# Delta-rule recurrence in chunks: three tiles for a's rows, and the preparation of the next chunks at another place in the order

## The chip, the cores and the metric

One core of a Trainium2 chip runs the whole program. The metric is the device time of one execution in microseconds (us), as the median of several runs. The engines are named as in the profile: PE (TensorE, with PEld for its weight loads), DVE (VectorE), ACT (ScalarE), POOL (GpSimd), SP (SyncE). SP's queue issues nearly all DMAs, one after the other: a DMA that waits for its buffer holds up those that stand behind it.

## The reference

```python
for t in range(S):                       # S = 768, 4 x 8 heads, head size 40
    y[:, :, t] = einsum('bhd,bhde->bhe', r_t, state)
    Sa = einsum('bhde,bhe->bhd', state, a_t)
    state = state * w_t[:, :, None, :] - einsum('bhd,bhe->bhde', Sa, b_t) \
          + einsum('bhd,bhe->bhde', v_t, k_t)
...
x = _moe_ref(y, ...)      # y as [4, 768, 320]: gelu, norm, a 768 x 768 mix over time, gate, + x
return _moe2_ref(x, ...)  # relu, a convolution of width 3, sigmoid gate, projection
```

All of it is float32. The change touches the recurrence alone (`_attn_ref`).

## The kernel before, in words

The recurrence is cut into 12 chunks of 64 steps. A chunk (`hg` in the code) is worked on for all 32 heads at once; the two halves of the heads (`q` = 0, 1) are independent chains. Two chunks make a group `g`, so there are six groups, and the loop over `g` at the end of `_attention` is the place of the change.

What is done for a chunk:

- `prep(hg)` loads a's rows (`at`, 1 MB), the rows of k and b (`kbt`, 1 MB) and the decays, makes running products of the decays by scans (L100, L103 on DVE), and scales `at` (L105, DVE) and `kbt` (L107, POOL) with them.
- `products(hg)` multiplies `kbt` by `at` on PE (`gk`, L129), masks the result into the tile `la` (L132, DVE), transposes `kbt` on PE (`pkb`, L135), copies that out (L136, ACT), and copies a part of `la` on POOL (L140).
- `solve_a(g)` inverts the triangular 32x32 blocks of both chunks of a group on DVE: two transposes of `la` into `mu` (L164), 30 steps of a multiplication and an addition that depend on each other (L171, L173), and two transposes out (`tn` L177, `tt` L179). These are called here solve 0 to solve 5. A solve needs `la` of both of its chunks.
- `solve_b(g, tq)` finishes the inverse for one chunk on PE (`pn` L192, `pt` L204, both of 32x32 tiles) and ACT (`n1` L198, `tt` L209), and at its end copies `at` into `la` (L210). Only then is that chunk's `at` tile free.
- `chain(g, c)` carries the state through one chunk and one half of the heads: `py` L227, `pz` L234, `pS` L243 and L246, `pzt` L255 on PE, with short copies on ACT (L231, L237, L258) and DVE (L236, L251, L252) between. `chain 2` needs `chain 0`, `chain 3` needs `chain 1`.
- `spart` transposes the state (`p` L265). `ypart` makes the output of one chunk and half: `gh` L279 and `pyo` L288, L290 on PE, `ghs` L283 and `xo` L293 on DVE, then the DMA to `x_attn`. `prep_y` and `prep_v` load what these need (`r`, `zv`, `vz`).

The list `ORDER` gives for every group in which order these pieces are written: `a` is a part of the next group's solve (three of the 30 steps), `b0`, `b1` the two `solve_b` of the next group, `p0`, `p1` and `g0`, `g1` `prep` and `products` of the two chunks of the group after the next, `sp` and `y` the parts of the same name, `py` a `prep_v`. A scheduler then orders the instructions of each engine by its own clock; of those that are ready it takes the higher `level` first (chains 3; a, b, sp, p and g 2; y 0). On each engine the instructions then run strictly in that order.

The tiles that matter: `at` comes from the pool `e2` with two buffers, `mu` and `n1` from `e1` with one each, `la` is a pair (`la_103`, `la_104`) that the groups use in turn. So `prep` of a chunk can load `at` only when `solve_b` of the chunk two before it has copied its own out.

After the six groups the rest of the network follows from about 770 us on; it isn't touched.

Of the kernel before, what the change touches and what calls it, by code (L numbers as in the profile page):

```python
# [10 lines left out]
F32 = mybir.dt.float32  # L11
# [16 lines left out]
def _attention(ctx, tc, ident, gu, wp, wr, a, kb, r, vt, v, x):  # L28
# [6 lines left out]
    D, C, J = 40, 64, 4  # L35
# [11 lines left out]
    e1 = early.enter_context(tc.tile_pool(name="a_e1", bufs=1, side="right"))  # L47
    e2 = early.enter_context(tc.tile_pool(name="a_e2", bufs=2, side="right"))
# [30 lines left out]
    def flat(t):  # L79
        return t.rearrange("p n t -> p (n t)")  # L80

    def prep(hg):

        at = e2.tile([128, 16, 2, C], F32, name="at")
        kbt = e1.tile([128, 16, 2, C], F32, name="kbt")
        px = p4.tile([128, 16, 65], F32, name="px")
        ws = [[], []]
        for q in range(2):
            for i, src in enumerate((wp, wr)):
                t = e2.tile([128, 8, 65], F32, name=f"w{i}")  # L90
                nc.sync.dma_start(out=flat(t), in_=src[hg, :, 520 * q:520 * q + 520])
                ws[q].append(t)
            if q == 0:
                nc.sync.dma_start(out=at.rearrange("p n P t -> p (n P t)"), in_=a[hg])
                nc.sync.dma_start(out=kbt.rearrange("p n c t -> p (n c t)"), in_=kb[hg])
        for q in range(2):
            ns = slice(8 * q, 8 * q + 8)
            w1, w2 = ws[q]
            nc.vector.memset(first[:, :, 0], 1.0)  # L99
            nc.vector.tensor_tensor_scan(out=flat(px[:, ns]), data0=flat(w1), data1=flat(first), initial=0.0,  # L100
                                         op0=ALU.mult, op1=ALU.add)
            nc.vector.reciprocal(first[:, :, 0], px[:, ns, 64])
            nc.vector.tensor_tensor_scan(out=flat(w2), data0=flat(w2), data1=flat(first), initial=0.0,  # L103
                                         op0=ALU.mult, op1=ALU.add)
            nc.vector.tensor_tensor(out=at[:, ns], in0=at[:, ns], in1=px[:, ns, None, 0:C].to_broadcast([128, 8, 2, C]),  # L105
                                    op=ALU.mult)
            nc.gpsimd.tensor_tensor(out=kbt[:, ns], in0=kbt[:, ns],  # L107
                                    in1=w2[:, :, C - 1::-1][:, :, None, :].to_broadcast([128, 8, 2, C]), op=ALU.mult)
            for i, t in enumerate((flat(px[:, ns]), flat(w2))):
                junk = e1.tile([128, 8 * 65], F16, name="junk")  # L110
                u = 4 * hg + 2 * q + i
                nc.scalar.activation(out=junk, in_=t, func=AF.Square, scale=2.0 ** -32, accum_out=gu[:, u:u + 1])
        tl[hg] = dict(px=px, at=at, kbt=kbt)
# [70 lines left out]
    def solve_b(g, tq):  # L184

        la, tt, tn = (grp[g][n] for n in ("la", "tt", "tn"))
        cs = slice(4 * tq, 4 * tq + 4)
        pn = ps_a.tile([128, 4, J, 32], F32, name="pn", tag="pa")
        for c in range(4):
            for j in range(J):  # L190
                for P in range(2):
                    nc.tensor.matmul(out=pn[rq(2 * P + 1), c, j], lhsT=la[rq(2 * P), P, 4 * tq + c, j, 32:64],  # L192
                                     rhs=tn[rq(2 * P), 4 * tq + c, j], start=True, stop=True,
                                     tile_position=(64 * P, 64 * P + 32))
        n1 = e1.tile([128, 4, J, 32], F32, name="n1")
        for P in range(2):
            i1 = rq(2 * P + 1)
            nc.scalar.activation(out=n1[i1], in_=pn[i1], func=AF.Copy)  # L198
        pt = ps_a.tile([128, 4, J, 32], F32, name="pt", tag="pa")
        for c in range(4):  # L200
            for j in range(J):
                for P in range(2):
                    i0, i1 = rq(2 * P), rq(2 * P + 1)
                    nc.tensor.matmul(out=pt[i0, c, j], lhsT=n1[i1, c, j], rhs=tt[i1, 4 * tq + c, j, 32:64],  # L204
                                     start=True, stop=True, tile_position=(64 * P + 32, 64 * P))
        at = tl[2 * g + tq]["at"]
        for P in range(2):
            i0 = rq(2 * P)
            nc.scalar.activation(out=tt[i0, cs, :, 32:64], in_=pt[i0], func=AF.Copy)  # L209
            nc.scalar.activation(out=la[half[P], P, cs].rearrange("p c j t -> p (c j) t"), in_=at[half[P], :, P],  # L210
                                 func=AF.Copy, scale=-1.0)
# [59 lines left out]
    def ypart(g, c4):  # L271
        hg, q = 2 * g + c4 // 2, c4 % 2
        d = tl[hg]
        kbn, px, (r2, zv) = d["kbn"], d["px"], rv[2 * hg + q]
        pyo = ps_a.tile([128, 8, C], F32, name="pyo", tag="pa")
        for s in range(2):
            gh = ps_g.tile([128, J, 2, C], F32, name="gh", tag="pg")
            for j in range(J):
                nc.tensor.matmul(out=gh[:, j].rearrange("p P t -> p (P t)"),  # L279
                                 lhsT=zv[:, 4 * s + j].rearrange("p c t -> p (c t)"),  # L280
                                 rhs=r2[:, 4 * s + j].rearrange("p P t -> p (P t)"), start=True, stop=True)
            ghs = p2.tile([128, J, 2, C], F32, name="ghs")
            nc.vector.tensor_tensor(out=ghs, in0=gh, in1=m8, op=ALU.mult)  # L283
            for j in range(J):
                for P in range(2):
                    i = 4 * s + j
                    if hg > 0:
                        nc.tensor.matmul(out=pyo[half[P], i], lhsT=s0s[hg, q][:, D * i:D * i + 64], rhs=r2[:, i, P],  # L288
                                         start=True, stop=False)
                    nc.tensor.matmul(out=pyo[half[P], i], lhsT=kbn[:, 8 * q + i, P], rhs=ghs[:, j, P],  # L290
                                     start=(hg == 0), stop=True)
        xo = p2.tile([128, 2, J, C], F32, name="xo")
        nc.vector.tensor_tensor(out=xo.rearrange("p s j t -> p (s j) t"), in0=pyo, in1=px[:, 8 * q:8 * q + 8, 0:C],  # L293
                                op=ALU.mult)
        for s in range(2):
            xv = x[2 * q + s, :, C * hg:C * hg + C].rearrange("(j P e) t -> P e j t", j=J, P=2)
            for P in range(2):
                nc.sync.dma_start(out=xv[P], in_=xo[real[P], s])

    def level(n):  # L300
        return tc.high_priority(offset=100000 * n)
# [16 lines left out]
    for hg in (2, 3):  # L318
        prep(hg)
        products(hg)  # L320
    ORDER = ["chain 0", "chain 1", "a", "a", "sp 0", "a", "y 0", "a", "a", "sp 1", "a", "py0", "y 1", "a", "a", "chain 2",
             "chain 3", "a", "a", "a", "b0", "p0", "sp 2", "y 2", "b1", "py1", "g0", "sp 3", "y 3", "p1", "g1"]
    for g in range(NG):
        n1, n2 = g + 1 < NG, g + 2 < NG
        sa = solve_a(g + 1) if n1 else iter(())
        if not n1:
            early.close()
        for it in ORDER:
            if it == "a":
                with level(2): next(sa, None)  # L330
            elif it in ("b0", "b1"):
                if n1:
                    with level(2):
                        run(sa)
                        solve_b(g + 1, int(it[1]))
            elif it in ("p0", "p1"):
                if n2:
                    with level(2): prep(2 * g + 4 + int(it[1]))
            elif it in ("g0", "g1"):
                if n2:  # L340
                    with level(2): products(2 * g + 4 + int(it[1]))
            elif it in ("py0", "py1"):
                if n1: prep_v(2 * g + 2 + int(it[2]))
            else:
                what, c = it.split()
                c = int(c)
                last = 2 * g + c // 2 == NH - 1
                if what == "chain":
                    with level(3): chain(g, c)
                    if not n1 and c == 1:  # L350
                        yield
                elif what == "sp":
                    if not last:
                        with level(2): spart(g, c)
                else:
                    ypart(g, c)
                    if 4 * g + c + 3 < 2 * NH: prep_y(4 * g + c + 3)


# [443 lines left out]
```

## Time and profile before

| | |
|---|---|
| median of 3 runs | 1268.96 us (1262.32 to 1287.53) |
| the profiled execution | 1269.13 us, of which the span from first to last instruction is 1267.4 us |
| busy share of the span | PE 76%, PEld 69%, DVE 58%, ACT 34%, POOL 18% |
| mean granted PE clock | 0.793 of full |
| recurrence | about 0 to 770 us |

The profile shows one execution on the engines' common time axis. A row of the timeline gives start, duration, engine, line, operation, the tiles as out<-in, the count of equal instructions merged, and in brackets the idle time of that engine just before and what ended it. A matmul of float32 appears twice in the counts of the trace (two passes). The clock PEclk is the share of PE's full clock that was granted, at either of two levels, 1.2 and 2.4 GHz.

### The profile page before, as it was taken

Reading aid. Unit: us, or ns where it says so; the run is one execution under the profiler, and the core shown is the slowest. Engines: PE = TensorE matmul, PEld = TensorE weight load, DVE = VectorE, ACT = ScalarE, POOL = GpSimd, SP = SyncE. Lnnn points to the kernel's source line nnn. Section 1 sums busy time; section 2 is a strip of 40 time slices with the busy share of each in tenths; the row PEclk is TensorE's granted clock in tenths of the full one; section 3 lists DMA queues with packets and bytes.
Section 4 is the critical chain, followed back from the end, with each engine's and each line's share of the span. In section 5 each row is a group of like instructions: output and inputs, shape, how many; then the busy total and the mean of one; then the engine's idle time right before and its main releaser. Section 6 shows DMA issues by size and latency. Waiting matters only on the chain.

```text
span 1267.4 us, 23131 instructions
## 1 busy us (share of the span) xinstructions
PE 957.5 (76%) x9777; PEld 870.8 (69%) x9777; DVE 730.5 (58%) x1323; ACT 429.2 (34%) x833; POOL 228.4 (18%) x213
## 2 busy tenths in 40 slices
PE   3218719990997399819994886589999978899995
PEld 3217717880776288717883785589999968799994
DVE  5873682189247622772285534285555668767763
ACT  2214212230432213212221423242222336777763
POOL 4300210021101100220020101230111143333331
PEclk8658955685878557855885588989999989899997
DMA  9302501352235113510430327200000121000000
GB/s 307 123 16 105 162 27 35 108 161 76 76 116 162 59 35 114 155 47 32 137 95 28 118 72 218 70 27 1 1 1 1 34 74 60 16 17 32 17 18 33
DMA packets 47490, 94.49 MB, mean 75 GB/s; under 512 B 20240, under 2 KB 26384, under 8 KB 44304
## 3 DMA queue, kind: packets, MB, share of 16 engines
q1 hardware_dynamic: 47376, 92.91, 23.2%
q8 instruction: 79, 1.29, 0.4%
q14 instruction: 35, 0.29, 0.1%
HBM read 85.02 MB, written 7.86 MB: 73 GB/s over the span
## 4 chain that ended last, share of the span: by engine, by line
PE 26%; DVE 11%; DMA 7%; ACT 6%; issue 3%; POOL 3%; SPq 0%; DVEq 0%; POOLq 0%; ACTq 0%
PE pv L612 5%; PE pr L633 3%; DMA raw<-in_moe_w_in 2%; PE pq L703 2%; PE pu L594 2%; DMA raw<-in_moe_w_out 2%; PE ph L563 2%; POOL cv L689 2%; DVE cv L684 2%; DVE gl L693 2%; ACT cv L683 1%; DVE cv L686 1%; DMA raw<-in_moe_w_sg 1%; PE gk L129 1%; PE p L680 1%
## 5 line engine op out<-in xcount | busy, mean ns | idle before, releaser
L192 PE MATMUL pn<-tn,la 32*32 32x32 f32 x768 | 35.0, 234 | 173.7 <-DVE tn L177 173.7
L192 PEld LDWEIGHTS pn<-tn,la 32*32 32x32 f32 x768 | 26.8, 145 | 184.3 <-issue 163.0
L129 PE MATMUL gk<-at,kbt 128*128 128x128 f32 x384 | 89.2, 372 | 32.3 <-POOL kbt L107 22.2
L129 PEld LDWEIGHTS gk<-at,kbt 128*128 128x128 f32 x384 | 69.4, 256 | 43.5 <-POOL kbt L107 26.6
L107 POOL TENSOR_TENSOR kbt<-kbt,w 128x1024 f32<-128x1024 f32 x24 | 56.3, 2351 | 235.3 <-DVE first L99 139.9
L689 POOL TENSOR_TENSOR cv<-cv,hz 128x384 f32<-128x384 f32 x64 | 61.8, 974 | 123.5 <-ACT cv L688 123.5
L171 DVE TENSOR_TENSOR mtmp<-mu 128x30 f32<-128x30 f32 (+9 forms) x180 | 74.2, 412 | 5.3
L132 DVE TENSOR_TENSOR la<-gk,minus 128x512 f32<-128x512 f32 x48 | 32.9, 685 | 72.9 <-PE gk L129 72.9
L210 ACT ACTIVATE la<-at 64x1024 f32<-64x1024 f32 x24 | 25.3, 1054 | 143.1 <-issue 104.0
L105 DVE TENSOR_TENSOR at<-at,px 128x1024 f32<-128x1024 f32 x24 | 35.2, 1488 | 52.0 <-DMA at<-in_c_a 52.0
L612 PE MATMUL pv<-sg_hi,vh 128*128 128x384 f32 x192 | 64.4, 336 | 0.4 <-ACT vh L586 0.4
L612 PE MATMUL pv<-sg_lo,vh 128*128 128x384 f32 x192 | 64.4, 335 | 0.0
L173 DVE TENSOR_TENSOR mu<-mu,mtmp 128x30 f32<-128x30 f32 (+9 forms) x180 | 61.2, 340 | 5.3
L612 PE MATMUL pv<-sg_hi,vl 128*128 128x384 f32 x192 | 64.1, 335 | 0.0
L290 PE MATMUL pyo<-ghs,kbn 128*64 128x64 f32 x768 | 62.3, 245 | 2.1 <-DVE ghs L283 2.1
L258 ACT ACTIVATE zv<-pzt 64x512 f32<-64x512 f32 x48 | 28.3, 590 | 102.8 <-PE pzt L255 68.4
L255 PE MATMUL pzt<-tt,ys 128*128 128x64 f32 x384 | 60.8, 323 | 1.6 <-ACT s L268 1.6
L288 PE MATMUL pyo<-r,s 128*64 128x64 f32 x704 | 61.6, 251 | 0.0
L616 POOL TENSOR_TENSOR g<-g,u 128x384 f32<-128x384 f32 x32 | 35.2, 1103 | 140.1 <-DVE g L615 138.4
L255 PEld LDWEIGHTS pzt<-tt,ys 128*128 128x128 f32 x384 | 56.9, 234 | 4.4 <-ACT s L268 2.2
L703 PE MATMUL pq<-wv_hi,gh 128*128 128x320 f32 x192 | 42.3, 328 | 23.0 <-ACT gh L692 23.0
L290 PEld LDWEIGHTS pyo<-ghs,kbn 128*64 128x64 f32 x768 | 53.9, 158 | 5.9 <-DVE ghs L283 2.9
(149 smaller groups left out, 2469.1 us busy)
## 6 DMA issues: line engine op xcount, KB each, us to landing
at<-in_c_a SPq DMA_DIRECT2D x12, 1024.0 KB
kbt<-in_c_kb SPq DMA_DIRECT2D x12, 1024.0 KB
zv<-in_c_vt SPq DMA_DIRECT2D x24, 512.0 KB
r<-in_c_r SPq DMA_DIRECT2D x24, 512.0 KB
w<-in_c_wp SPq DMA_DIRECT2D x24, 260.0 KB
w<-in_c_wr SPq DMA_DIRECT2D x24, 260.0 KB
raw<-in_moe_w_in SPq DMA_DIRECT2D x8, 512.0 KB
vz<-in_c_v SPq DMA_DIRECT2D x24, 160.0 KB
```

Of the source, the lines that this page charges most:

```text
L107: nc.gpsimd.tensor_tensor(out=kbt[:, ns], in0=kbt[:, ns], in1=w2[:, :, C - 1::-1][:, :, None, :].to_broadcast([128, 8, 2, C]), op=ALU.mult)
L129: nc.tensor.matmul(out=pg[:, j].rearrange("p P t -> p (P t)"), lhsT=kbt[:, n].rearrange("p c t -> p (c t)"), rhs=at[:, n].rearrange("p P t ...
L171: nc.vector.tensor_tensor(out=tv, in0=mu[:, j + 1:32, j:j + 1].to_broadcast([128, n, j]), in1=mu[:, j:j + 1, 0:j].to_broadcast([128, n, j] ...
L173: nc.vector.tensor_tensor(out=mu[:, j + 1:32, 0:j], in0=mu[:, j + 1:32, 0:j], in1=tv, op=ALU.add)
L192: nc.tensor.matmul(out=pn[rq(2 * P + 1), c, j], lhsT=la[rq(2 * P), P, 4 * tq + c, j, 32:64], rhs=tn[rq(2 * P), 4 * tq + c, j], start=True, ...
L255: nc.tensor.matmul(out=pzt[:, i], lhsT=ys[:, i].rearrange("p P e -> p (P e)"), rhs=tt[:, 2 * c4 + i // 4, i % 4], start=True, stop=True)
L288: nc.tensor.matmul(out=pyo[half[P], i], lhsT=s0s[hg, q][:, D * i:D * i + 64], rhs=r2[:, i, P], start=True, stop=False)
L290: nc.tensor.matmul(out=pyo[half[P], i], lhsT=kbn[:, 8 * q + i, P], rhs=ghs[:, j, P], start=(hg == 0), stop=True)
L612: nc.tensor.matmul(out=po, lhsT=l[:, fs], rhs=rr[:, k, cs], start=(n == 0), stop=(n == 3 * NT - 1))
L633: nc.tensor.matmul(out=po, lhsT=ww[:, k, ms], rhs=ghl[k][i], start=(n == 0), stop=(n == 3 * NF1 - 1))
L689: nc.gpsimd.tensor_tensor(out=cv, in0=cv, in1=h[:, 1:N2 + 1], op=ALU.mult)
L703: nc.tensor.matmul(out=po, lhsT=gs[k][g][:, ts], rhs=rr[:, k], start=(n == 0), stop=(n == 3 * NF2 - 1))
```

## The change

`at` gets three buffers. `n1` gives up its own buffer and takes `mu`'s. In `ORDER` the first preparation of the group after the next (`p0`, `g0`) moves from behind the solve to its middle, before and behind chains 2 and 3; the second (`p1`) now follows `b0`, and `b1` comes last but one. `ypart` gets level 1 instead of 0.

```diff
-        at = e2.tile([128, 16, 2, C], F32, name="at")
+        at = e2.tile([128, 16, 2, C], F32, name="at", bufs=3)
...
-        n1 = e1.tile([128, 4, J, 32], F32, name="n1")
+        n1 = e1.tile([128, 4, J, 32], F32, name="n1", tag="mu")
...
-    ORDER = ["chain 0", "chain 1", "a", "a", "sp 0", "a", "y 0", "a", "a", "sp 1", "a", "py0", "y 1", "a", "a", "chain 2",
-             "chain 3", "a", "a", "a", "b0", "p0", "sp 2", "y 2", "b1", "py1", "g0", "sp 3", "y 3", "p1", "g1"]
+    ORDER = ["chain 0", "chain 1", "a", "a", "sp 0", "a", "y 0", "a", "a", "sp 1", "a", "py0", "y 1", "a", "p0", "chain 2",
+             "chain 3", "g0", "a", "a", "a", "a", "sp 2", "y 2", "b0", "p1", "sp 3", "py1", "y 3", "b1", "g1"]
...
-                    ypart(g, c)
+                    with level(1): ypart(g, c)
```

What the scheduler makes of it, at three places that repeat in each group.

First the stretch between two solves, here the one that follows solve 3. On PE, before, the 32x32 products `pn` of the second `solve_b` and the 128x128 products `gk` stand in turn, ahead of chain 1's `pz`:

```order
L227 MATMUL py<-vz,la_104 64x40 x16
L192 MATMUL pn<-tn,la_104 32x32 x6
L129 MATMUL gk<-at,kbt 128x128
L192 MATMUL pn<-tn,la_104 32x32
L129 MATMUL gk<-at,kbt 128x128
L192 MATMUL pn<-tn,la_104 32x32
L129 MATMUL gk<-at,kbt 128x128
L192 MATMUL pn<-tn,la_104 32x32
L129 MATMUL gk<-at,kbt 128x128
L192 MATMUL pn<-tn,la_104 32x32 x7
L129 MATMUL gk<-at,kbt 128x128
L234 MATMUL pz<-ys_106,tt_100 64x40 x16
```

On PE, now, at the same place:

```order
L255 MATMUL pzt<-tt_100,ys_105 128x64 x8
L192 MATMUL pn<-tn,la_104 32x32 x5
L246 MATMUL pS<-vz,kbn 64x40
L227 MATMUL py<-vz,la_104 64x40 x16
L246 MATMUL pS<-vz,kbn 64x40 x15
L192 MATMUL pn<-tn,la_104 32x32 x2
L234 MATMUL pz<-ys_106,tt_100 64x40
L192 MATMUL pn<-tn,la_104 32x32
L234 MATMUL pz<-ys_106,tt_100 64x40 x15
L243 MATMUL pS<-st_110,ident 64x320 x2
```

No `gk` stands there any more: 16 of the 32 `gk` of a group have moved into the solve before.

On DVE, in the same stretch, before, from chain 1's last copy to the scans of the second `prep`:

```order
L252 TENSOR_TENSOR st_110<-pS,px 128x320
L293 TENSOR_TENSOR xo<-pyo,px 128x512
L283 TENSOR_TENSOR ghs<-gh,mask 128x512 x2
L236 COPY vz<-pz 64x320
L251 TENSOR_TENSOR vz<-pS,px 64x320 x2
L252 TENSOR_TENSOR st_109<-pS,px 128x320
L293 TENSOR_TENSOR xo<-pyo,px 128x512
L100 SCALAR_TENSOR_TENSOR px<-w_3496,first 128x520
L102 RECIPROCAL first<-px 128x8
L105 TENSOR_TENSOR at<-at,px 128x1024
```

On DVE, now:

```order
L252 TENSOR_TENSOR st_110<-pS,px 128x320
L293 TENSOR_TENSOR xo<-pyo,px 128x512
L100 SCALAR_TENSOR_TENSOR px<-w_3345,first 128x520
L102 RECIPROCAL first<-px 128x8
L105 TENSOR_TENSOR at<-at,px 128x1024
```

One output part and chain 2's copies no longer stand ahead of the scans (L100).

Second the solve, on DVE. Before, its later steps follow each other:

```order
L171 TENSOR_TENSOR mtmp<-mu 128x238
L173 TENSOR_TENSOR mu<-mu,mtmp 128x14x17
L171 TENSOR_TENSOR mtmp<-mu 128x234
L173 TENSOR_TENSOR mu<-mu,mtmp 128x13x18
L171 TENSOR_TENSOR mtmp<-mu 128x228
```

Now, at the same steps:

```order
L171 TENSOR_TENSOR mtmp<-mu 128x238
L132 TENSOR_TENSOR la_104<-gk,minus 128x4x2x64
L173 TENSOR_TENSOR mu<-mu,mtmp 128x14x17
L171 TENSOR_TENSOR mtmp<-mu 128x234
L173 TENSOR_TENSOR mu<-mu,mtmp 128x13x18
L171 TENSOR_TENSOR mtmp<-mu 128x228
L132 TENSOR_TENSOR la_104<-gk,minus 128x4x2x64
```

Four of a group's eight `la` (L132) stand among the steps of the solve before, and wait there for `gk`; chain 3's copies, two L105, two more L283 and one more L293 do so too.

Third SP's queue. Before, both loads of `at` stand together, ahead of the second chunk's `kbt`:

```order
L91 DMA w_3504<-in_c_wr 128x520
L94 DMA at<-in_c_a 128x2048 x2
L146 DMA vz<-in_c_v 64x640 x2
L156 DMA r_3287<-in_c_r 128x1024
L298 DMA x_attn<-xo 40x4x64 x4
L155 DMA zv<-in_c_vt 128x1024
L95 DMA kbt<-in_c_kb 128x2048
```

Now, the second `at` and the `kbt` of the chunk that is prepared in the solve stand behind `r`, an output and the decays:

```order
L298 DMA x_attn<-xo 40x4x64 x4
L94 DMA at<-in_c_a 128x2048
L146 DMA vz<-in_c_v 64x640 x2
L156 DMA r_3449<-in_c_r 128x1024
L94 DMA at<-in_c_a 128x2048
L298 DMA x_attn<-xo 40x4x64
L91 DMA w_3919<-in_c_wp 128x520
L298 DMA x_attn<-xo 40x4x64 x3
L91 DMA w_3925<-in_c_wp 128x520
L91 DMA w_3921<-in_c_wr 128x520
L91 DMA w_3927<-in_c_wr 128x520
L95 DMA kbt<-in_c_kb 128x2048
```

The load of `r` waits for an output part on PE, so what stands behind it waits as well.

## Rows read from the trace of the kernel before

**Rows 1.** Stretches: window, length, PE, PEld, DVE, ACT, POOL busy, PEclk, DMA, GB/s

```profile
184.60:275.80 91.20, 86.56 (x1070) 73.91 (x1071) 29.72 (x44) 26.01 (x48) 9.83 (x8) 0.65 0.26 80
275.80:315.20 39.40, 10.26 (x196) 9.37 (x195) 37.58 (x81) 4.97 (x12) 4.40 (x2) 0.67 0.37 119
315.20:392.30 77.10, 72.65 (x1070) 62.43 (x1071) 29.76 (x44) 26.01 (x48) 9.82 (x8) 0.81 0.31 95
...
431.70:523.70 92.00, 87.04 (x1070) 74.22 (x1071) 29.85 (x44) 26.01 (x48) 9.83 (x8) 0.64 0.26 81
...
563.20:651.00 87.80, 83.65 (x1070) 71.29 (x1071) 30.98 (x43) 26.01 (x48) 9.83 (x8) 0.67 0.21 67
651.00:682.40 31.40, 12.40 (x213) 11.31 (x211) 29.41 (x73) 2.06 (x4) 0.00 (x0) 0.77 0.35 112
```

**Rows 2.** Timeline of DVE around the end of solve 3

```profile
429.84 1.91 DVE L177 STREAM_TRANSPOSE tn<-mu 128x1024 f32<-128x1024 f32 x1
431.65 1.91 DVE L179 STREAM_TRANSPOSE tt<-mu 128x1024 f32<-128x1024 f32 x1
442.14 2.36 DVE L105 TENSOR_TENSOR at<-at,px 128x1024 f32<-128x1024 f32 x2 [8.58 <-DMA at<-in_c_a]
445.74 0.48 DVE L236 COPY vz<-pz 64x320 f32<-64x320 f32 x1 [1.24 <-PE pz L234]
```

**Rows 3.** Timeline of DVE, later in that stretch, to the start of solve 4

```profile
491.81 0.69 DVE L293 TENSOR_TENSOR xo<-pyo,px 128x512 f32<-128x512 f32 x1 [16.25 <-PE pyo L290]
...
502.91 1.24 DVE L100 TENSOR_TENSOR_SCAN px<-w,first 128x520 f32<-128x520 f32 x1
...
523.67 1.95 DVE L164 STREAM_TRANSPOSE mu<-la 64x1024 f32<-64x1024 f32 x1
```

**Rows 4.** Timeline of PE in the same stretch

```profile
431.89 1.92 PE L192 MATMUL pn<-tn,la 32*32 32x32 f32 x64 [28.86 <-DVE tn L177]
434.97 0.44 PE L227 MATMUL py<-vz,la 128*64 128x40 f32 x2 [1.15 <-ACT la L210]
...
477.55 0.74 PE L204 MATMUL pt<-tt,n 32*32 32x32 f32 x20
478.22 0.43 PE L265 MATMUL p<-ident,st 128*64 128x40 f32 x2
478.59 0.31 PE L204 MATMUL pt<-tt,n 32*32 32x32 f32 x2
478.83 0.43 PE L265 MATMUL p<-ident,st 128*64 128x40 f32 x2
...
487.32 2.04 PE L265 MATMUL p<-ident,st 128*64 128x40 f32 x33
...
489.86 1.06 PE L135 MATMUL pkb<-ident,kbt 128*128 128x128 f32 x4
```

**Rows 5.** Groups of DVE from 184 to 684 us: busy us, mean ns, idle before

```profile
L105 DVE TENSOR_TENSOR at<-at,px 128x1024 f32<-128x1024 f32 x16 | 25.7, 1629 | 38.4 <-DMA at<-in_c_a 38.4
L132 DVE TENSOR_TENSOR la<-gk,minus 128x512 f32<-128x512 f32 x32 | 22.0, 688 | 63.0 <-PE gk L129 63.0
L283 DVE TENSOR_TENSOR ghs<-gh,mask 128x512 f32<-128x512 f32 x32 | 21.8, 682 | 13.7 <-PE gh L279 13.6
L251 DVE TENSOR_TENSOR vz<-pS,px 64x320 f32<-64x320 f32 x32 | 15.6, 489 | 30.9 <-PE pS L246 30.6
...
L252 DVE TENSOR_TENSOR st<-pS,px 128x320 f32<-128x320 f32 x16 | 7.9, 492 | 0.2
```

**Rows 6.** Waits of SP's queue, 184 to 684 us: total us, times, longest

```profile
SPq L94 <- ACT la L210: 205.8, 8, 31.8
SPq L156 <- PE pyo L290: 93.0, 14, 17.2
```

**Rows 7.** Timeline of PE just after solve 0

```profile
101.22 3.78 PE L129 MATMUL gk<-at,kbt 128*128 128x128 f32 x16 [5.53 <-DVE at L105]
```

**Rows 8.** The page: GB/s moved in each of 40 slices

```profile
GB/s 307 123 16 105 162 27 35 108 161 76 76 116 162 59 35 114 155 47 32 137 95 28 118 72 218 70 27 1 1 1 1 34 74 60 16 17 32 17 18 33
```

## Prediction

> **What bounds the kernel now.** I first cut the recurrence at the starts and ends of the solves and asked for the busy time of each engine in each piece [rows 1]. Two kinds of piece alternate. In the stretches between solves (91.2, 77.1, 92.0 and 87.8 us after solves 1 to 4) PE is busy nearly throughout: 86.56 of 91.2, 72.65 of 77.1, 87.04 of 92.0, 83.65 of 87.8. DVE has some 30 us of work there. In the solves (39.4 us; the last 31.4) it is the other way round: DVE is busy 37.58 of 39.4 and PE 10.26, and the timeline of PE has one gap of 28.86 us before the `pn` that wait for `tn` [rows 4]. So the time is the sum of two bounds in turn: PE's queue, in order, in a stretch, and DVE's chain of steps in a solve. A microsecond of PE work that moves from a stretch into a solve is worth a microsecond, as long as PE's gap there holds it. A microsecond of DVE work that moves with it costs one.
>
> The largest waits by name don't say this. DVE waits 38.4 us for the DMA of `at` over the four stretches [rows 5], 8.58 at a time [rows 2], but PE has work in its queue then [rows 4], so this idle time isn't on the path. In SP's queue the loads of `at` stand 205.8 us behind L210's copy [rows 6]; that is only how long a buffer is held.
>
> The stretches differ by clock: the share granted is 0.65, 0.81, 0.64, 0.67 [rows 1], so in three of four PE runs at 1.2 GHz for most of the stretch, after its gap in the solve.
>
> **The change, part by part.** I make the sum against the profiled 1269.13 us (span 1267.4 and 1.7 outside), which is the median of the runs shown within 0.2 us.
>
> *The four stretches.* Three things go from PE's queue ahead of chain 1's first `xo` (L293, 491.81 us, 60 us after `tn` [rows 3]).
> First, 16 `gk`. The 16 passes after solve 0 took 3.78 us, or 0.236 each [rows 7]; 16 `gk` are 32 passes, 7.6 us.
> Second, 37 of 61 changes to or from 32x32 tiles, counted in PE's order up to there. Where `pt` and `p` alternate, two of each take 0.61 us from start to start (478.22 to 478.83); in rows they take 2.04/33 and 0.74/20, so 0.198 for the same four [rows 4]. The excess of 0.41 is for two changes: 0.2 each, 7.4 us.
> Third, 4 `pkb`: 1.06 us [rows 4].
> Together 16 us where PE is at the lower clock; I estimate 12 at the higher one, where the 7.6 and the 1.06 shrink by about half.
> Then, from that `xo` to the scans (L100, 502.91), DVE's order has another `xo`, two `ghs` and chain 2's copies, each behind PE: 11.1 us [rows 3]. Now the scans stand right behind the first `xo` (0.69 us), so 10.4 us go. From the scans to the next `mu` 20.8 us pass [rows 3]; the same `gk` and `la` of the second chunk must still be made there, with chain 2's copies in place of chain 3's. I add 2 (0 to 6 if the clock is low there).
> So 16 + 10.4 − 2 = 24 us a stretch, 96 for four. The low end is 62 (12 each, and half of the 10.4 given to other waits, less 2), the high end 110 (no added 2, and 1.5 more for `pn` that also stand apart).
> That `n1` takes `mu`'s tile costs nothing: `mu`'s last reader, `tt` L179, began at 431.65 and takes 1.91 [rows 2]; the copy into `n1` waits for `pn`, which lasts to 433.8, and then for L210's, until which PE waits at 434.97 [rows 4]. If it did bind, it would be for a microsecond in each stretch.
>
> *DVE's work in the solves.* It goes straight onto a DVE that is busy 37.58 of 39.4 us [rows 1]. Four L132 at 0.688, two L105 (1.18 alone; 1.6 in the mean; say 1.2 each), two `ghs` at 0.682, one `xo` at 0.69, and chain 3's four copies (0.48, two of 0.489, 0.49) [rows 2, 3, 5]: 2.75 + 2.4 + 1.36 + 0.69 + 1.95 = 9.1 us. For solves 1 to 4: 36.4. Solve 0 gets the four L132 (2.75), the last one chain 3 and some `ghs` (2.6). Sum +41.8, with ends 36 and 48: some of it fits into the 1.8 us of idle time a solve has, and L105 beside POOL's L107 took up to 2.9 when paired.
>
> *Waits in the solve.* No solve of before shows a `gk`, so this cost is bounded. An L132 that stands ahead of its `gk` stops the steps behind it. Nothing is the low end: PE has 28.9 us free [rows 4], the 7.6 us of `gk` need 7.6 of them, and chain 3 some 5. The high end is the wait of L132 on `gk` in the stretches: 63.0 us over 32, 2 us each [rows 5], so 8 a solve, and 10 with chain 3. I take 2 a solve in five solves: +10 (0 to 50). It is nearer to nothing, since the 2 us were measured on a PE that was full.
>
> *The start.* After solve 0 PE waits 5.53 us for L105 and then makes 16 passes of `gk` in 3.78 [rows 7]; both now lie in solve 0, 9.3 us. One more `at` (1 MB) is loaded at the beginning, when the queues move 307 GB/s [rows 8]: 3.4 us, if the first solve waits for it. Net −5.9 (−9 to +5).
>
> *After the solves.* The last stretch has the same work for chain 0 to 3 of the last group; `y` at level 1 only moves outputs among themselves: 0 (±6).
>
> **Sum:** −96 + 41.8 + 10 − 5.9 = −50; 1269 − 50 = **1219 us**. Its own range, from the ends that are likely together, is 1195 to 1243.
>
> **The rivals.**
>
> *PE keeps the higher clock* (faster than the forecast). With `gk` and chain 3 in the solve, PE's gap is shorter, and the stretches may start at 2.4 GHz. One stretch shows what this is worth: 77.1 us at 0.81 against 91.2, 92.0 and 87.8 [rows 1]; three times down to 77.1 is 14.1 + 14.9 + 10.7 = 40: 1179. For it: the gap shrinks from 28.9 to maybe 10 us. Against it: PE is busy almost without a pause in the stretches and is granted the lower clock for most of each all the same, so a long row of work alone doesn't bring it back. The Trainium skill ("TensorE: Matmul & The Clock Gate", What's actually happening) says that activity releases the throttle soon after PE resumes; by it nearly all of a stretch would already be at full speed before and the change could gain little here. The trace doesn't agree: busy 86.56 of 91.2 at 0.65 [rows 1].
>
> *The gain and the cost nearly cancel* (within 2%, which is about what a measurement of this kernel can tell from no change). If all four stretches come out at 71 us, that is 91.2 less 20, because what is left in them runs at the lower clock from end to end, the gain is 20 + 6 + 21 + 17 = 64 in place of 96. With waits of 0.5 to 8 us a solve (2 to 40 in all) the sum is −64 + 41.8 − 5.9 + 2 to 40 = −26 to +12: 1243 to 1281. For it: the lower clock is already the rule in three of four. Against it: the work that leaves is the part that PE did at its worst.
>
> *SP's queue makes the solve wait* (slower). The `kbt` of the in-solve chunk stands in SP's queue behind `r`, outputs and four `w`. The load of `r` waits for `pyo`: 93.0 us over 14 times, 17.2 at the longest [rows 6]. If such a wait falls into the solve, `kbt` comes late, L107 and L105 after it, `gk` after these, and the L132 among the steps stop all steps behind them: DVE then stands as it did for the DMA of `at`, 8.58 us [rows 2], but now on the path. It decides where a solve loses over 15 us beyond the 9.1: −96 + 41.8 − 5.9 + 4 × 15 = 0, and slower by 2% from 22. At 25 us a solve in solves 1 to 4: 1269 − 60 + 100 = 1309. Against it: with three tiles the second `at` no longer waits for L210, and `r` waits for a `pyo` of the output part before, which PE makes early in the stretch.
>
> That the change doesn't do what it says I leave out: four `la` of the later group do stand among the steps in DVE's order.
>
> **How the numbers follow.** Forecast 0.56 (1195 to 1243), higher clock 0.14 (about 1179), near cancelling 0.20, SP's queue 0.10. The forecast is the likeliest. The range leaves out the slow rival's 0.10, a quarter of the fast one's and a third of the near case's, 0.20 in all: from 1174, since the fast rival is some 10 us wide to either side, to 1268. Faster by over 2% (below 1243.6) is 0.56 + 0.14 = 0.70, within 2% 0.20, slower 0.10.
>
> **What would show it.** In the windows of the changed kernel the stretches after solves 1 to 4 should be 53 to 71 us, with PE busy throughout; a length near 77 or above says that the 24 is wrong. A solve from L164 to `tn` should take 48 to 53 us, DVE busy in nearly all of it: idle DVE ahead of an L132, by `gk`, above 2 us in one solve says that the waits were too small, and the releaser says whether PE or a DMA is behind it. `gk` should stand inside the solve, and PE's longest gap there be under 15 us. In SP's queue the wait of L156 tells the slow rival: its `kbt` would land after the solve's middle. PEclk near 0.8 or above in all four stretches tells the fast one. The prediction would be wrong above all if DVE's order in the solve has work that PE can't supply in time, or if the scans' new place only moves DVE's wait to the second chunk's L132, which still follow PE's whole queue.

## The result, and the profile after

The changed kernel takes 1191.45 us in the median of 4 runs (1175.90 to 1211.70), beside 1266.43 us for the kernel before. The ratio is 0.930, with a 95% interval of 0.924 to 0.937: 7% faster, where 2% is about what a measurement of this kernel can tell from no change. Some runs, two of these four and the profiled one of this kernel's repetition below among them, were disturbed, and the ratios and stretches here and below leave them out, which is why a ratio can differ from that of the medians. The profiled execution took 1175.90 us (span 1174.1), 93.2 less than the one before.

The busy time of the changed kernel by stretch and solve, in order of time (window, length, then PE, PEld, DVE, ACT, POOL busy, PEclk, DMA, GB/s), the counterpart of [rows 1]:

```profile
93.00:153.20 60.20, 55.93 (x894) 51.43 (x895) 15.92 (x26) 22.74 (x39) 7.61 (x6) 0.68 0.22 74
153.20:197.90 44.70, 19.84 (x220) 17.05 (x218) 43.05 (x89) 6.95 (x16) 5.89 (x4) 0.83 0.50 165
197.90:251.60 53.70, 48.07 (x812) 42.77 (x813) 20.81 (x29) 21.98 (x40) 8.41 (x6) 0.73 0.26 81
251.60:300.00 48.40, 32.79 (x460) 29.12 (x456) 45.44 (x94) 8.87 (x20) 5.87 (x5) 0.88 0.49 158
300.00:354.60 54.60, 48.97 (x826) 43.53 (x827) 20.79 (x29) 22.74 (x42) 8.61 (x6) 0.73 0.28 87
354.60:401.50 46.90, 31.33 (x440) 28.29 (x438) 45.11 (x94) 8.01 (x18) 5.67 (x4) 0.89 0.49 154
401.50:453.00 51.50, 45.83 (x812) 41.24 (x814) 20.87 (x31) 21.98 (x40) 8.43 (x6) 0.77 0.27 86
453.00:501.40 48.40, 32.77 (x460) 29.10 (x455) 45.46 (x94) 8.87 (x20) 5.86 (x5) 0.88 0.50 158
501.40:551.70 50.30, 43.46 (x814) 38.56 (x814) 22.19 (x30) 21.99 (x40) 8.44 (x6) 0.81 0.14 44
551.70:591.00 39.30, 23.64 (x410) 20.98 (x406) 33.18 (x80) 3.74 (x8) 0.15 (x1) 0.89 0.38 116
```

Two columns tell the story. The passes of PE in a stretch after solves 1 to 4 went from 1070 to 812 to 826, and those in solves 2 to 4 from 196 or 197 to 440 or 460: a quarter of a stretch's work now runs under DVE's solve. And PEclk in the stretches is 0.73 to 0.81, where three of four had 0.64 to 0.67. The four stretches fell from 348.1 to 210.1 us; the six solves grew from 223.1 to 265.0, since DVE has the added work there (45.44 busy of 48.40 us in solve 2).

The timeline of PE around the end of solve 3, the counterpart of [rows 4]:

```profile
377.97 2.08 PE L129 MATMUL gk<-at,kbt 128*128 128x128 f32 x8 [7.91 <-POOL kbt L107]
...
384.70 2.08 PE L129 MATMUL gk<-at,kbt 128*128 128x128 f32 x8 [2.39 <-POOL kbt L107]
...
401.65 1.92 PE L192 MATMUL pn<-tn,la 32*32 32x32 f32 x64 [4.68 <-DVE tn L177]
```

The `gk` stand in the solve, and PE's gap of 28.86 us has become three longer ones of 7.91, 2.39 and 4.68 us. DVE in the same stretch, the counterpart of [rows 3]:

```profile
430.82 0.69 DVE L293 TENSOR_TENSOR xo<-pyo,px 128x512 f32<-128x512 f32 x1 [5.87 <-PE pyo L290]
431.55 1.24 DVE L100 TENSOR_TENSOR_SCAN px<-w,first 128x520 f32<-128x520 f32 x1
...
453.00 3.92 DVE L164 STREAM_TRANSPOSE mu<-la 64x1024 f32<-64x1024 f32 x2
```

The first `xo` comes 29.3 us after the solve's end in place of 60.1, the scans 0.73 us behind it in place of 11.1, and the next `mu` 21.5 us behind the scans (20.8 before). Groups of DVE and waits of SP from 197.9 to 591 us, for [rows 5, 6]:

```profile
L105 DVE TENSOR_TENSOR at<-at,px 128x1024 f32<-128x1024 f32 x14 | 23.4, 1668 | 0.0
L132 DVE TENSOR_TENSOR la<-gk,minus 128x512 f32<-128x512 f32 x28 | 19.2, 685 | 9.2 <-PE gk L129 9.0
```

```profile
SPq L156 <- PE pyo L290: 40.5, 12, 7.5
SPq L94 <- ACT la L210: 39.9, 7, 14.7
```

The DMA wait of L105 is gone, the wait of L132 on `gk` fell from 63.0 to 9.0 us, and in SP's queue `r` and `at` wait less than half as long.

### The profile page after: what moved, and what is told of

Read it like the earlier page. It is cut to its first block, busy times and chain, and to the rows that moved or that the text cites. A ratio compares the mean times of both kernels' runs of the same rounds, so it can differ in the third digit from the quotient of the medians.

```text
span 1174.1 us, 23127 instructions
## 1 busy us (share of the span) xinstructions
PE 915.6 (78%) x9777; PEld 845.9 (72%) x9777; DVE 725.1 (62%) x1323; ACT 428.7 (37%) x833; POOL 229.3 (20%) x213
## 3 DMA queue, kind: packets, MB, share of 16 engines
q8 instruction: 79, 1.29, 0.5%
## 5 line engine op out<-in xcount | busy, mean ns | idle before, releaser
L129 PE MATMUL gk<-at,kbt 128*128 128x128 f32 x384 | 76.4, 354 | 91.7 <-POOL kbt L107 86.7
L129 PEld LDWEIGHTS gk<-at,kbt 128*128 128x128 f32 x384 | 67.1, 259 | 97.9 <-POOL kbt L107 90.0
L192 PE MATMUL pn<-tn,la 32*32 32x32 f32 x768 | 29.4, 223 | 63.3 <-DVE tn L177 63.3
L192 PEld LDWEIGHTS pn<-tn,la 32*32 32x32 f32 x768 | 23.1, 136 | 68.8 <-issue 66.5
L279 PE MATMUL gh<-r,zv 128*128 128x128 f32 x384 | 63.0, 300 | 5.8 <-DMA r<-in_c_r 3.2
L288 PE MATMUL pyo<-r,s 128*64 128x64 f32 x704 | 64.3, 251 | 1.7 <-DVE xo L293 1.7
L251 DVE TENSOR_TENSOR vz<-pS,px 64x320 f32<-64x320 f32 x44 | 21.5, 488 | 66.6 <-PE pS L246 49.9
L279 PEld LDWEIGHTS gh<-r,zv 128*128 128x128 f32 x384 | 50.7, 199 | 10.4 <-DVE la L132 3.3
L288 PEld LDWEIGHTS pyo<-r,s 128*64 128x64 f32 x704 | 53.0, 156 | 6.9 <-issue 1.7
L693 DVE TENSOR_TENSOR gl<-cv,gh 128x384 fp32r<-128x384 f32 x64 | 42.2, 659 | 24.7 <-ACT gh L692 24.7
L236 DVE COPY vz<-pz 64x320 f32<-64x320 f32 x24 | 11.6, 482 | 74.1 <-PE pz L234 73.6
```

The lines of the kernel that those rows point to most:

```text
L129: nc.tensor.matmul(out=pg[:, j].rearrange("p P t -> p (P t)"), lhsT=kbt[:, n].rearrange("p c t -> p (c t)"), rhs=at[:, n].rearrange("p P t ...
L693: nc.vector.tensor_tensor(out=gl, in0=cv, in1=gh, op=ALU.subtract)
```

## The experiments

The times below are ratios to the kernel before on the same chip, with their 95% intervals; its median was 1256.74 us beside the first four, 1265.97 beside the next four and 1259.97 beside the last four, on three chips. Clocks and lengths of stretches are those of one profiled execution of each kernel. The first theory, from the prediction: work leaves PE's queue in the stretches. Its first rival: PE keeps the higher clock because its gap in the solve is shorter. A second one, from the profile after: PE has fewer turns between 32x32 tiles and others, and that is where the clock comes from.

**The tile without the order.** The third `at` and `n1` on `mu`'s tag, old `ORDER`, `ypart` at level 0.

```diff
-        at = e2.tile([128, 16, 2, C], F32, name="at")
+        at = e2.tile([128, 16, 2, C], F32, name="at", bufs=3)
-        n1 = e1.tile([128, 4, J, 32], F32, name="n1")
+        n1 = e1.tile([128, 4, J, 32], F32, name="n1", tag="mu")
```

> The kernel before with the third tile for a's rows and n1 on mu's tag alone; ORDER and the levels are the old ones. With the third tile the scheduler itself puts four L132 of the later group into the solve. If the tile carries the gain, the stretches after solves 1 to 4 are 50 to 60 us in place of 77 to 92, the solves 45 to 50, and the time is 1175 to 1205 us. If the places in ORDER carry it, the stretches stay above 75 us and the time is above 1250 us.

Measured: 0.955 (0.951 to 0.960), median 1199 us. Stretches of 60.3, 64.4, 60.2, 60.2 us, a little longer than expected, and solves 1 to 4 of 43.7 to 44.3. The row of the third:

```profile
410.20:470.40 60.20, 54.69 (x1022) 47.94 (x1023) 24.67 (x37) 26.10 (x48) 8.62 (x6) 0.84 0.35 112
```

So the tile alone makes most of the gain: the scheduler moves the products into the solve by itself once the buffer is there. PE has only 48 passes fewer in the stretch (1070 to 1022), which are 16 `gk` of two passes each and 16 passes of `gh`; the stretch is 32 us shorter all the same, and its PEclk is 0.84. The changes to or from 32x32 tiles in the whole program have fallen from 296 to 96.

**Solve_b at the highest level, nothing moved.**

```diff
-                    with level(2):
-                        run(sa)
-                        solve_b(g + 1, int(it[1]))
+                    with level(2): run(sa)
+                    with level(4): solve_b(g + 1, int(it[1]))
```

> The kernel before with solve_b at the highest level, so that pn and pt stand in PE's queue in one piece instead of in turn with gk and p: 46 changes to or from 32x32 tiles in the whole program in place of 296. If a change costs 0.2 us, 250 fewer are 50 us, of which the stretches after solves 1 to 4 have some 45: 1220 to 1235 us. If the changes are hidden or the chain, which now waits behind pn, takes it back, 1260 to 1275 us.

Measured: 0.940 (0.935 to 0.945), median 1181 us. That is far below what 0.2 us a change gives. The stretches are 67.8, 65.7, 62.7 and 63.0 us with all their work in them, and the solves as before. The third stretch and the solve after it, and two rows from PE's timeline at its start:

```profile
396.30:459.00 62.70, 57.53 (x1069) 52.49 (x1070) 29.64 (x42) 25.99 (x48) 9.82 (x8) 0.87 0.36 117
459.00:498.60 39.60, 10.36 (x197) 9.46 (x195) 37.79 (x81) 4.98 (x12) 4.40 (x2) 0.69 0.36 118
```

```profile
396.45 1.92 PE L192 MATMUL pn<-tn,la 32*32 32x32 f32 x64 [28.87 <-DVE tn L177]
...
405.77 1.29 PE L192 MATMUL pn<-tn,la 32*32 32x32 f32 x64
```

PE's gap is the old one (28.87 us), the passes are the old 1069, and yet PEclk is 0.87 in place of 0.64 and the stretch 29 us shorter. A row of 64 `pn` takes 1.92 us at the lower clock and 1.29 where it has risen in between. So the gap alone doesn't decide the clock of the stretch, and work need not leave it. The edit changes more than the turns, though: level 4 also puts `solve_b` ahead of the chains (level 3), and no run separates the two.

**The gap filled.** Products of 128x320, whose results nothing reads, in PE's queue during the solve of the kernel before.

```diff
+    def filler(n):
+        if True:
+            pf = ps_c.tile([128, 8, D], F32, name="pf", tag="pc")
+            for i in range(n):
+                nc.tensor.matmul(out=pf.rearrange("p n e -> p (n e)"), lhsT=ident, rhs=rst(0)[:, 0:8 * D], start=True, stop=True)
...
+                if na == 10 and n1: filler(36)
```

> The kernel before with 36 added products of 128x320 per group, of which nothing is read; some 30 of them stand in PE's queue right ahead of the pn that wait for the solve, so that PE's gap of 28.9 us there is partly filled. The recurrence's own work is all there. If the clock that PE is granted in the stretches falls because of that gap, the stretches at 0.64 to 0.67 come near the one at 0.81 (77 us): 30 to 40 us less, 1225 to 1240 us. If the clock has nothing to do with the gap, PEclk of the stretches stays near 0.65 in three of four and the time is 1265 to 1285 us.

Measured: 0.991 (0.982 to 1.000). PE still waits up to 12.1 us ahead of `pn`, so the gap is more than halved, not closed, and the time is in neither of the ranges expected. A stretch, then a solve and the stretch behind it, twice:

```profile
181.80:257.20 75.40, 70.99 (x1036) 61.13 (x1037) 29.78 (x44) 25.99 (x48) 9.66 (x8) 0.81 0.30 93
257.20:296.40 39.20, 30.39 (x302) 23.82 (x300) 37.53 (x81) 4.97 (x12) 4.61 (x3) 0.95 0.40 129
296.40:389.30 92.90, 87.37 (x1042) 74.74 (x1043) 29.75 (x43) 26.00 (x48) 9.82 (x8) 0.64 0.24 75
389.30:428.40 39.10, 29.30 (x296) 22.84 (x295) 37.46 (x81) 4.98 (x12) 4.43 (x2) 0.92 0.40 130
428.40:519.50 91.10, 86.94 (x1036) 74.21 (x1037) 29.73 (x43) 25.99 (x48) 9.66 (x8) 0.62 0.25 77
```

The solves run at 0.92 to 0.95, and the stretches behind them at 0.62 and 0.64 as before; the two others, of 75.4 and 75.6 us, had 0.81 and 0.82, where the kernel before had one such stretch. So a shorter gap alone doesn't secure the clock.

**Turns and rows as filler.** Both in the kernel with `solve_b` at the highest level: `small` is a product of 32x32, `wide` one of 128x40, in turn, or in three rows.

```diff
+        for i in range(44):
+            small(i)
+            wide(i)
```

```diff
+        for i in range(80): wide(i)
+        for i in range(80): small(i)
+        for i in range(40): wide(i)
```

> The kernel before with solve_b at the highest level, and 44 pairs of added products per group, of which nothing is read: one of 32x32 and one of 128x40 in turn, most of them in PE's queue ahead of pn, in its gap in the solve. The recurrence's own work is all there. If such turns keep the clock down, the solves show PE busy for some 20 us more and yet a PEclk of 0.5 to 0.7, and the first 15 us of the stretch stay at the lower clock. If only the gap keeps it down, PEclk in the solves rises above 0.85.

> As the one with pairs in turn, but 80 of 128x40, 80 of 32x32 and 40 of 128x40 in rows: as much added PE time with two changes of tile. If the turns keep the clock down, PEclk in the solves is above 0.85 here. If small products as such keep it down, it stays below 0.75 here too.

Measured: 0.988 (0.983 to 0.993) with turns and 0.957 (0.945 to 0.969) with rows, where the level alone had 0.940. Solves 2 to 4 show PEclk 0.65 to 0.67 with turns and 0.78 to 0.79 with rows. First a piece of the turns in the first kernel, then of the rows in the second, each with PE busy throughout:

```profile
395.20:410.50 15.30, 15.30 (x102) 11.70 (x102) 6.37 (x11) 2.19 (x6) 4.42 (x2) 0.50 0.18 55
```

```profile
379.90:394.60 14.70, 14.70 (x244) 14.51 (x242) 13.68 (x27) 1.46 (x4) 2.97 (x2) 0.64 0.22 57
```

In this piece the turns run at the lower clock from end to end. The piece of rows comes to 0.64, and it has two parts: the row of 32x32 had 0.84 (379.8 to 385.9 us), the row of 128x40 behind it 0.50 (385.9 to 394.6, PE busy 8.70 of 8.70 us). That second row isn't like those of the kernel: a pass takes 0.11 us there and 0.062 in a row of `p` [rows 4]. So the second rival holds in one direction: 15 us of turns, without a gap, didn't raise the clock, while solves 2 to 4 with 128x320 products had 0.92 to 0.95. But the row of 128x40 did no better without turns.

Nor do the turns in the solve lower the clock of the stretch behind it: with turns the stretches are 64.6 to 69.1 us at 0.79 to 0.87, with the level alone 62.7 to 67.8 at 0.82 to 0.87. What the turns cost lies in solves 1 to 5, 248.9 us in place of 189.2, where DVE's `ghs` waits for `gh` behind them. That the turns alone decide isn't shown.

**Parts of the order.** First p0 and g0 in the solve, the rest behind it as it was:

```diff
...
-             "chain 3", "g0", "a", "a", "a", "a", "sp 2", "y 2", "b0", "p1", "sp 3", "py1", "y 3", "b1", "g1"]
+             "chain 3", "g0", "a", "a", "a", "a", "b0", "sp 2", "y 2", "b1", "py1", "sp 3", "y 3", "p1", "g1"]
```

> The changed kernel with p0 and g0 in the middle of the solve as now, but b0, b1, p1 and g1 behind it in the old order. If what moves into the solve carries the gain, the time is that of the changed kernel within 1%: 1170 to 1190 us. If the new place of p1 and b1 has a part in it, the stretches are longer by 5 us or more each, and the time is above 1195 us.

Measured: 0.948 (0.941 to 0.954), median 1192 us. The stretches are 57.6, 56.3, 58.3 and 66.9 us: the new place of p1 and b1 is worth some 7 us a stretch on top (16.6 of the 29 in all are in the last, which is at 0.70 here), of which the solves take 3 back. This order has 98 changes of tile, about as many as the tile alone (96), and nearly its ratio.

Then p1 and b1 alone, p0 and g0 behind the solve (ahead of chain 2 an `a` takes p0's place again):

```diff
...
-             "chain 3", "g0", "a", "a", "a", "a", "sp 2", "y 2", "b0", "p1", "sp 3", "py1", "y 3", "b1", "g1"]
+             "chain 3", "a", "a", "a", "sp 2", "y 2", "b0", "p0", "g0", "p1", "sp 3", "py1", "y 3", "b1", "g1"]
```

> The changed kernel with p0 and g0 behind the solve, but p1 after b0 and b1 last but one as now. In PE's order pn still stand in turn with p, 202 changes to or from 32x32 tiles in place of 152. If the time goes with the work that stands in the solve, which here has the four L132 too, the stretches are 50 to 57 us and the time is within 1.5% of the changed kernel. If the turns decide, the stretches are 58 to 72 us and PEclk below 0.75 in most of them: 1195 to 1225 us.

Measured: 0.984 (0.975 to 0.992), median 1231 us, above both ranges expected. The stretches are 67.7, 70.1, 67.1 and 69.9 us. The second of them:

```profile
312.60:382.70 70.10, 66.50 (x918) 57.82 (x918) 22.85 (x34) 25.80 (x47) 7.63 (x6) 0.65 0.28 90
```

Here 152 passes have left the stretch and the four L132 stand in the solve, and the gain is the smallest of the kernels that move work: with 202 changes of tile left, PEclk is 0.65 to 0.73. Beside the tile with the old order (48 passes moved, 96 changes, 0.78 to 0.84) this is the clearest sign that the order on PE counts for more than how much is moved. It is a sign, not a proof: the two orders differ in more than their turns.

**The level of the output part.**

```diff
-                    with level(1): ypart(g, c)
+                    ypart(g, c)
```

> The changed kernel with ypart at level 0 again. If the level only orders outputs among themselves, as the prediction has it, the time is that of the changed kernel within 1%, 1165 to 1190 us, and the stretches stay at 50 to 55 us. If the level has a part in the gain, the output parts fall back into the stretches, which are then 58 us or more, and the time is above 1195 us.

Measured: 0.961 (0.951 to 0.972), median 1210 us, stretches of 72.1, 59.9, 59.9, 60.1 us. One of them:

```profile
317.80:377.70 59.90, 54.94 (x897) 48.40 (x898) 22.15 (x33) 23.38 (x43) 7.63 (x6) 0.73 0.27 83
```

At level 0 some 70 to 86 passes fall back from the solve into a stretch (897 against 812 to 826). They are not `gh` and `pyo` but chain 3's `pz`, `pS` and `pzt`, with a few `py`: our reading, which no run tests, is that the outputs, let through earlier, had made room for the chain.

**Both.** The highest level for `solve_b` in the kernel with the tile alone, and in the changed one (the same edit as above).

> The kernel before with the third tile, n1 on mu's tag and solve_b at the highest level; the old ORDER. 46 changes of tile, four L132 in the solve. Beside the run with the level alone (0.940 of before, stretches 63 to 68) this shows what work moved into the solve is worth without turns. If it is a microsecond for a microsecond less DVE's part, as the sum had it, the stretches fall by some 12 us, the solves grow by 5: 0.92 of before or less. If most of the third tile's gain was turns, 0.93 to 0.945.

Measured: 0.956 (0.950 to 0.962), outside both ranges expected, no better than the tile alone and worse than the level alone. The solves cost 18.5 us more than with the level alone (176.2 against 157.7, four of them), the time to solve 1 another 10.6, and the stretches gave back 8: 59.2, 57.9, 64.8 and 69.2 us at 0.79, 0.82, 0.71 and 0.67. Here, with 46 changes of tile, the clock is low in two stretches, so few turns don't secure it either.

> The changed kernel with solve_b at the highest level: 46 changes to or from 32x32 tiles in the program in place of the 152 left by the change. If taking pn and pt out of turns is a gain of its own beside the work that moves into the solve, the stretches fall from 50 to 55 us to 45 to 50 and the time to 1145 to 1165 us. If both are the same gain, counted once, the time stays within 1% of the changed kernel, 1165 to 1190 us.

Measured: 0.928 (0.919 to 0.937), median 1166 us. The changed kernel, run again beside the same on another chip:

> The changed kernel as it is, beside the others on one chip: 0.93 of before, stretches 50 to 55 us.

> The changed kernel with solve_b at the highest level, on the same chip as the changed kernel. If it is better than the change, by the turns of pn with p that the change has left, it is 0.5 to 1.5% below it; if both take the same gain, the two agree within 0.5%.

Measured: 0.940 (0.932 to 0.948) for the change and 0.925 (0.918 to 0.931) with the level, medians 1183 and 1155 us. The intervals all but touch; the difference of 1.5% is on the side of the level. The stretch after solve 1 in the first and in the second run of the kernel with the level, which were on two chips:

```profile
199.90:261.00 61.10, 55.55 (x890) 50.62 (x890) 20.70 (x32) 22.68 (x42) 8.62 (x6) 0.63 0.23 71
```

```profile
199.20:248.00 48.80, 43.06 (x890) 39.30 (x891) 20.83 (x34) 22.70 (x42) 8.61 (x6) 0.84 0.29 89
```

The same 890 passes in the same order take 61.1 us at 0.63 and 48.8 at 0.84: 12.3 us for the clock, with nothing in the code changed. It isn't the chip: in the first run itself the other three stretches, of 889 or 890 passes, take 49.1 to 49.4 us at 0.83. From these numbers PE's work takes some 1.7 times as long at the lower clock: an estimate, since a PEclk of 0.63 means 26% of 61.1 us at the higher clock and 0.84 means 68% of 48.8.

## Why the prediction was right, and where it was off

The forecast was 1219 us, with 1195 to 1243 as its own range. The profiled execution took 1175.9 and the median is 1191.45: both lie below that, and inside the whole range of 1174 to 1268, the first by 2 us. The room for them came from the rival of the higher clock (about 1179, chance 0.14), whose reason was wrong; that the range held is in part luck. The gain is 93 us in place of 50. The mechanism held: PE's queue bounds the stretches, DVE the solves, and work crossed from the one to the other. What was missing is mostly the clock, as far as the stretches show it. The sizes, step by step:

- *Four stretches, −96 (−62 to −110).* Measured −138, past the high end. The stretch that was at 0.81 before gave 22.5 us, where 24 was forecast; the three at 0.64 to 0.67 gave 37.5 to 40.5. In the stretch after solve 3 the three pieces are −30.8 up to the first `xo` (16 forecast), −10.4 from there to the scans (10.4), and +0.7 to the next `mu` (2). So the term that was too small is the 16. It left out that 64 passes of `pt` would fall behind the `xo`, and it reckoned at one clock. The group of `pt` up to the first `xo`, before and after:

```profile
L204 PE MATMUL pt<-tt,n 32*32 32x32 f32 x128 | 8.5, 240 | 0.5 <-ACT n L198 0.5
```

```profile
L204 PE MATMUL pt<-tt,n 32*32 32x32 f32 x64 | 2.4, 238 | 0.5 <-ACT n L198 0.5
```

That is 6.1 us, turns included; in rows 64 passes are 2.4 (0.74/20 each [rows 4]). Then the clock. Before, PE was busy 57.17 of the first 59.0 us at the lower level all through; after, it rose 10.2 us into the stretch:

```profile
431.70:490.70 59.00, 57.17 (x630) 47.34 (x630) 10.89 (x16) 13.88 (x22) 3.28 (x4) 0.50 0.12 42
```

```profile
401.50:411.70 10.20, 8.46 (x194) 7.87 (x194) 1.79 (x2) 5.32 (x8) 2.06 (x2) 0.50 0.32 109
411.70:428.70 17.00, 17.00 (x332) 14.63 (x329) 3.90 (x8) 4.09 (x8) 0.00 (x0) 1.00 0.08 22
428.70:442.40 13.70, 9.77 (x154) 9.25 (x148) 10.54 (x12) 9.16 (x18) 4.58 (x2) 0.50 0.59 187
```

Two rows of the same trace, the first at the lower clock, the second at the higher one, show what it is worth:

```profile
120.27 3.68 PE L255 MATMUL pzt<-tt,ys 128*128 128x64 f32 x16
413.77 2.00 PE L255 MATMUL pzt<-tt,ys 128*128 128x64 f32 x16
```

By that ratio of 1.8, or the 1.7 from the 890 passes above, the 17.0 us would be 29 to 31 at the lower clock: an estimate of 12 to 14 of the 30.8 us for the clock here. With the 2.4 of `pt` that leaves 14 to 16 for the work and the turns, which is about the forecast 16. The clock falls again at 428.7, behind the last `pn` in turn with `p`. The Trainium skill ("TensorE: Matmul & The Clock Gate", What's actually happening) lets activity release the throttle. The trace agrees after the change in this stretch, where the rise comes 10.2 us in, and not before, where PE was as busy and had turns.
- *Changes of tile at 0.2 us.* As a duration the rows were right, but the kernel with the level alone, which has 250 fewer, gained 75 us (0.940): 0.3 us each if all of it is put down to them, the clock that came back and the place ahead of the chains included.
- *DVE's work in the solves, +41.8, and waits, +10 (0 to 50).* Solve 0 to 5 grew by 2.9, 5.7, 9.0, 7.5, 8.9 and 7.9, together 41.9, waits included. In solves 1 to 4 DVE is idle 1.7 to 3.0 us, 1.8 before; so the low end of the waits was right there. The last solve grew by 7.9, not 2.6: chain 3's passes and output parts came into it too, and DVE is idle for 6.1 of its 39.3 us.
- *The start, −5.9 (−9 to +5).* It cost 4.7: 2.7 us up to solve 0, and the stretch behind it is 60.2 us in place of 58.2, although 9.3 us of idle time and `gk` left its head. The clock took that back: it rose 38.8 us into that stretch, after 17.6 before:

```profile
93.00:131.80 38.80, 34.55 (x559) 31.98 (x560) 8.09 (x12) 16.70 (x27) 2.06 (x2) 0.50 0.23 82
```

```profile
87.40:105.00 17.60, 9.82 (x212) 9.14 (x214) 4.89 (x5) 7.75 (x10) 2.06 (x2) 0.50 0.34 121
```

Turns don't explain this one. From 111.7 to 131.8 us PE was busy 20.10 of 20.10 us without a single 32x32 product, and the clock stayed at 0.50; before, it rose right behind the row of 16 `gk` passes [rows 7] that has now moved. This stretch has six changes of tile in every kernel here (ten where turns were added), and it had 0.67 to 0.69 in all seven kernels with the third tile and 0.78 to 0.87 in all five without.

- *After the solves, 0.* Measured −1.9. But that level 1 "only moves outputs among themselves" is wrong: it lets 70 to 86 passes of chain 3 into a solve, and without it the kernel is at 0.961.
- *The DMA wait of `at` not on the path.* Right as far as the runs tell: it is gone, and the kernel with the level alone still has it, 39.7 us over the four stretches (38.4 before [rows 5]), and gained 6% all the same.
- *The rivals.* The higher clock came, in part: 0.73, 0.73, 0.77, 0.81. Its reason, the shorter gap, was wrong: a gap more than halved gave 0.9%, and with the gap as it was the level alone had 0.82 to 0.87. The near cancelling took the lower clock for granted from end to end. SP's queue did little: the load of `r` waits 7.5 us at most, and in the last solve alone PE's `gh` stands 2.63 us behind it.

Of the signs named ahead, the `gk` inside the solve and PE's longest gap up to a solve's end (12.5 us, under 15) came out; two stretches (51.5 and 50.3 us) and two solves (44.7 and 46.9 us) were shorter than said.

What stays open is what decides the clock of a stretch. The order on PE seems to have a large part in it, but the same code had 0.63 in one run and 0.84 in another, 46 changes of tile came with 0.87 as well as with 0.67, and the stretch after solve 0 stayed low without turns. How the gain of 138 us divides into work moved and clock is therefore settled for one stretch, and as an estimate, not for the whole.

The best kernel here is the change with `solve_b` at the highest level: 0.928 and 0.925 on two chips, 1.5% ahead of the change on the one chip where both ran.

## What to carry to other kernels

When an engine that works in order bounds a stretch, look not only at how much stands in its queue but at how it is mixed: raising the level of the 32x32 products, which puts them in one piece, was worth about as much (0.940) as the buffer and the new order together (0.930 and 0.940). Such gains need not add: the level and the buffer together came to 0.956. A buffer that lets a load start earlier may be all that a scheduler needs; try it before writing a new order by hand. And where the granted clock differs between stretches of the same code, carry two prices for each piece of PE work, and say which one a term uses.

## What was not expected of the hardware

- PE was busy 15.30 of 15.30 us with 32x32 and 128x40 products in turn and was granted the lower clock throughout; with products of 128x320 in the solve of the kernel before, three solves had 0.92 to 0.95.
- After the change, PE was busy 20.10 of 20.10 us behind solve 0 with no 32x32 product at all, and was granted the lower clock throughout.
- The same 890 passes had a PEclk of 0.63 or 0.84 in two runs on two chips, 12.3 us apart; three more stretches of the first run had 0.83.
